# Loading the query weights before the two gMLP weights in a decode-attention kernel

## The chip, the cores and the metric

One core of one Trainium2 chip. The time is the device time of the program in microseconds (us), lower is better. Most executions of one kernel agree within 0.3%, that is about 2 us here.

In this text PE (or TensorE) is the matmul engine, DVE the vector engine, ACT the scalar engine, POOL the engine that here writes a few constants and then only passes on semaphores, and SP the engine whose queue issues the loads. "Load engines" are the 16 DMA engines among which every large load is split.

## The reference, cut to what matters

```python
x = A_x                                             # 1 x 1 x 512
g = sigmoid((x * gate_w).sum(-1))
q = x @ wq                                          # wq: 512 x 4096, 32 heads of 128
scores = q . k_cache * Dh**-0.5                     # k_cache: 32 heads x 16384 x 128
a = (softmax(scores) @ v_cache) @ wo                # v_cache as large; wo: 4096 x 512
z = gelu(x @ w_in)                                  # w_in: 512 x 1792
z1, z2 = halves of z;  z2 = layernorm(z2)
b = (z1 * (w_sp * z2 + b_sp)) @ w_out               # w_out: 896 x 512
out = g * a + (1 - g) * b
```

Everything is bfloat16. The two caches are 134 MB each and all of them must come through the loads once; the arithmetic on one query token is small beside that.

## The kernel before

There are three buffers of 8.4 MB in SBUF. The caches are taken in 16 pairs of heads, K0 to K15 and V0 to V15, each one load of 128 rows of 64 KiB (K0, K15 and V15 are cut into pieces). They go into the buffers in turn, in the order K0, K1, V0, K2, V1, K3, V2 and so on, and load n waits until load n - 3 has been used up. The three setup weights lie in the third buffer, so that V0's load has to wait until the setup is done.

```python
# the small loads, on ACT's queue
act.op(... x_row <- A_x ...); act.op(... gw_row <- gate_w ...)
act.op(... wb_row[0] <- B_w_sp ...); act.op(... wb_row[1] <- B_b_sp ...)
# the setup weights, on SP's queue, ahead of K0
sp.op(lambda e: e.dma_start(out=w_in, in_=B_w_in.rearrange("(p c) f -> p (c f)", c=DC)), inc=(ld_w, 16))
sp.op(lambda e: e.dma_start(out=w_out, in_=B_w_out.rearrange("(p k) n -> p (k n)", k=FhC)), inc=(ld_u, 16))
sp.op(lambda e: e.dma_start(out=wq, in_=A_wq.rearrange("(p c) n -> p (c n)", c=DC)), inc=(ld_q, 16))
# ... (cut) x broadcast, gate, clears of PSUM
dve.op(lambda e: e.memset(ps_all[:, 0:7 * 512], 0.0), mark=True)

# PE's order in the setup:
#   1 gate             waits for the small loads
#   2 gMLP input       waits for ld_w      (pe_gmlp)
#   3 gMLP statistics  waits for DVE, which masks, sums (3.3 us) and squares the result of 2
#   4 queries          waits for ld_q      (pe_queries)
#   5 gMLP output      waits for ld_u      (pe_mixer); its end frees the setup buffer for V0
# ... (cut)

# the loads: load n waits for the user of load n - 3
k_at = [max(2 * i - 1, 0) for i in range(NP)]
v_at = [min(2 * i + 2, 2 * NP - 1) for i in range(NP)]
for n, kind, i in loads:
    wait = [user[n - 3]] if n >= 3 else [w_free] if buf[n % 3] is setup else []
    ...
# user of K_i: the exponentials of pair i (ACT), after DVE's four multiplications by the query
# and PE's sums of the products. user of V_i: PE's product with the probabilities.
```

So K0's end releases K2's load, and K1's end releases V1's load.

The softmax here doesn't subtract the row's maximum and nothing guards it: scores larger than these inputs give would overflow.

## Time and profile before

| | before |
|---|---|
| time, median of 3 runs | 654.57 us (653.9 to 655.1) |
| load queue busy, share of 16 load engines | 99.3% |
| PE, DVE busy | 63%, 52% |
| gMLP input weights landed, first gMLP matmul | 7.6 us, 8.6 us |
| V0's load issued / K0's first multiplication | 31.1 us / 32.2 us |
| V1's load issued | 84.9 us |

The page of the profile of the kernel before: the span, the busy time of the engines, the load queue (packets, MB, share of 16 engines' span), the group of DVE's multiplications (busy us and mean ns; idle time before them and what ended it), and the three setup loads (KB, us from issue to landing).

```profile
span 652.6 us, 7678 instructions
...
PE 412.8 (63%) x2354; PEld 46.3 (7%) x1326; DVE 339.3 (52%) x162; ACT 43.5 (7%) x112; POOL 2.1 (0%) x9
...
q1 hardware_dynamic: 6772, 279.58, 99.3%
...
L560 DVE TENSOR_TENSOR bufs<-bufs,qb x64 | 281.5, 4419 | 168.7 <-DVEq L84 168.7
...
bufs<-in_A_wq_dram SPq DMA_DIRECT2D x1, 4096.0 KB, 18.1
...
bufs<-in_B_w_in_dram SPq DMA_DIRECT2D x1, 1792.0 KB, 7.6
...
bufs<-in_B_w_out_dram SPq DMA_DIRECT2D x1, 896.0 KB, 8.8
```

The load queue is the limit: 99.3% against 63% for the busiest other engine. DVE sits idle for 169 us before its multiplications, in waits for semaphores; the view of waits counts 16 of them, as many as there are K loads.

The timeline of the kernel before, in order: start and duration in us, engine, line, operation, count, and in brackets the idle time before it and what ended it. DVE L312 makes the gate's product, PE L342 starts the gMLP's input, PE L104 with xb is the queries, SP L621 issues cache loads (V0 at 31.13, K2 at 59.38, V1 at 84.87), DVE L560 is the multiplication of K by the query (K0 at 32.20, K2 at 97.33).

```profile
6.86 0.41 DVE L312 TENSOR_TENSOR xg_row<-x_row,gw_row 1x512 bf16<-1x512 bf16 x1 [0.28 <-DMA wb_row<-in_B_b_sp_dram]
...
8.63 0.55 PE L342 MATMUL ps_all<-bufs,xb 128*128 x1
...
23.55 6.61 PE L104 MATMUL ps_all<-bufs,xb 128*64 x32
...
31.13 0.33 SPq L621 DMA_DIRECT2D bufs<-in_A_v_cache_dram  x1
32.20 8.76 DVE L560 TENSOR_TENSOR bufs<-bufs,qb  x2 [0.68 <-DVEq L84]
...
59.38 0.33 SPq L621 DMA_DIRECT2D bufs<-in_A_k_cache_dram  x1
...
84.87 0.33 SPq L621 DMA_DIRECT2D bufs<-in_A_v_cache_dram  x1
...
97.33 8.76 DVE L560 TENSOR_TENSOR bufs<-bufs,qb  x2 [13.12 <-DVEq L84]
```

DVE had been idle for 13.12 us when K2 arrived: at that place the engines are ahead of the loads.

### The profile page before, as it was taken

What the parts mean: (1) busy time and instruction counts of PE and PEld (TensorE: products, weight loads), DVE (VectorE), ACT (ScalarE), POOL (GpSimd) and SP (SyncE); (2) the same over time, 40 slices, a digit from 0 to 9 for tenths busy, and PEclk for the clock granted to TensorE, in tenths of its full rate; (3) what the DMA queues carried; (4) which work ended last, traced back from release to release, by engine and by line L of the source; (5) the groups of instructions that cost most, each with busy time, mean ns of one, the idle gap of its engine ahead of it and who ended that gap; (6) DMA issues with size and microseconds to landing.
All of it is one profiled execution on the core that took longest, in us unless ns stands there. A gap on an engine that the chain in (4) does not pass through costs nothing. (4 is left out here: it accounts for less than half of the span.)

```text
span 652.6 us, 7678 instructions
## 1 busy us (share of the span) xinstructions
PE 412.8 (63%) x2354; PEld 46.3 (7%) x1326; DVE 339.3 (52%) x162; ACT 43.5 (7%) x112; POOL 2.1 (0%) x9
## 2 busy tenths in 40 slices
PE   3455756757376674847657485674738657487767
PEld 0100010000101000010100101000010100001012
DVE  4596708356280745628166470925638083565600
ACT  2101010000001000010100001000010100001011
POOL 1000000000000000000000000000000000000000
PEclk9588986868889687888958789795887979688888
DMA  9999999999999999999999999999999999999997
GB/s 390 444 428 450 438 438 410 450 438 434 414 450 438 426 422 450 438 426 422 446 442 426 422 446 442 426 422 446 434 426 430 446 434 418 438 418 462 414 412 288
DMA packets 6781, 279.60 MB, mean 428 GB/s; under 512 B 760, under 2 KB 1020, under 8 KB 1532
## 3 DMA queue, kind: packets, MB, share of 16 engines
q1 hardware_dynamic: 6772, 279.58, 99.3%
q8 instruction: 1, 0.02, 0.0%
q10 hardware_dynamic: 8, 0.00, 0.0%
HBM read 279.58 MB, written 0.00 MB: 428 GB/s over the span
## 5 line engine op out<-in xcount | busy, mean ns | idle before, releaser
L560 DVE TENSOR_TENSOR bufs<-bufs,qb x64 | 281.5, 4419 | 168.7 <-DVEq L84 168.7
L89 PE MATMUL ps_all<-bufs,ident 128*128 x960 | 268.7, 438 | 0.0
L477 PE MATMUL ps_all<-bufs,ident 128*128 x64 | 28.9, 451 | 152.6 <-PEq L84 152.6
L104 PE MATMUL ps_all<-bufs,p_t 128*8 x1024 | 79.3, 388 | 53.0 <-PEq L84 52.9
L544 DVE TENSOR_REDUCE s_sb<-ps_all 128x64 f32<-128x512 f32 x64 | 44.1, 689 | 98.1 <-DVEq L84 98.1
L573 ACT ACTIVATE p_t<-s_sb 64x256 f32 (+1 forms) x32 | 13.3, 414 | 442.0 <-ACTq L84 441.6
L477 PEld LDWEIGHTS ps_all<-bufs,ident 128*128 128x128 bf16 x64 | 6.3, 99 | 373.3 <-issue 373.3
L104 PEld LDWEIGHTS ps_all<-bufs,p_t 128*8 x1024 | 17.2, 82 | 163.6 <-issue 163.6
L511 PE MATMUL ps_all<-pick,d_sb 128*128 128x2 f32 x128 | 16.8, 253 | 14.8 <-PEq L84 14.8
L511 PEld LDWEIGHTS ps_all<-pick,d_sb 128*128 128x128 f32 x128 | 15.5, 191 | 26.3 <-issue 26.3
L582 ACT COPY d_sb<-ps_all 128x512 f32<-128x512 f32 x16 | 9.4, 586 | 103.7 <-ACTq L84 103.7
L463 PE MATMUL ps_all<-zero,ident 128*128 128x512 bf16 x25 | 10.4, 415 | 0.0
L89 PE MATMUL ps_all<-zero,ident 128*128 128x512 bf16 x32 | 9.5, 379 | 0.0
L587 ACT CAST ps_all<-zero 128x512 f32<-128x512 bf16 x15 | 8.8, 589 | 1.7
L104 PE MATMUL ps_all<-bufs,xb 128*64 x32 | 6.6, 604 | 0.1
L377 PE MATMUL ps_all<-stats,const-float32-1.0 128*128 128x2 f32 x2 | 0.6, 364 | 9.2 <-DVE stats L375 9.2
L656 DVE TENSOR_TENSOR o_sb<-ps_all,rl 128x32 bf16<-128x32 f32 x1 | 0.2, 192 | 11.5 <-PE ps_all L511 11.5
L573 ACT ACTIVATION_READ_ACCUMULATOR p_t<-s_sb (+1 forms) x32 | 5.9, 184 | 0.0
L653 DVE RECIPROCAL rl<-ps_all 128x32 f32<-128x32 f32 x1 | 0.4, 358 | 10.5 <-PE ps_all L532 10.5
L354 DVE TENSOR_TENSOR bufs<-ps_all,ident 128x896 f32<-128x896 f32 x2 | 2.1, 1086 | 4.6 <-PE ps_all L89 4.6
L319 PE MATMUL ps_all<-xgw,const-float32-1.0 1*128 1x3 f32 x2 | 0.6, 358 | 6.1 <-DVE xgw L315 6.1
L89 PE MATMUL ps_all<-bufs,xb 128*128 x12 | 4.4, 494 | 0.0
(73 smaller groups left out, 44.4 us busy)
## 6 DMA issues: line engine op xcount, KB each, us to landing
bufs<-in_A_k_cache_dram SPq DMA_DIRECT2D x4, 4096.0 KB, 34.0
bufs<-in_A_v_cache_dram SPq DMA_DIRECT2D x1, 5120.0 KB, 33.2
bufs<-in_A_wq_dram SPq DMA_DIRECT2D x1, 4096.0 KB, 18.1
bufs<-in_A_wo_dram SPq DMA_DIRECT2D x3, 1024.0 KB, 23.5
bufs<-in_A_v_cache_dram SPq DMA_DIRECT2D x1, 2048.0 KB, 37.8
bufs<-in_B_w_in_dram SPq DMA_DIRECT2D x1, 1792.0 KB, 7.6
bufs<-in_A_v_cache_dram SPq DMA_DIRECT2D x1, 1024.0 KB, 39.8
bufs<-in_B_w_out_dram SPq DMA_DIRECT2D x1, 896.0 KB, 8.8
```

Source lines behind the costliest of these rows:

```text
L89: ins = eng.matmul(out, lhsT=lhsT, rhs=rhs, **flags).ins
L104: ins = eng.matmul(bank[0:m, 0:n], lhsT=lhsT, rhs=rhs, **flags).ins
L319: g_ok = pe.op(lambda e: e.matmul(l_ps[:, 0:3], lhsT=ones_f[0:1, :], rhs=xgw[:, :], start=True, stop=True), wait=[xgw_ok], mark=True)
L354: dve.op(lambda e, h=h, zh=zh: e.tensor_tensor(out=zm[:, 2 * h * ZB:2 * (h + 1) * ZB].rearrange("p (b m k) -> p b m k", b=2, k=FhC), in0=z ...
L463: e.matmul(args[0], lhsT=args[1], rhs=args[2], **flags)
L477: matmul_on(nc, e, lambda: e.matmul(s3, lhsT=ident[:, :], rhs=k3[:, :, 0:W], start=True, **flags), [(kw, 0)])
L511: ins = e.matmul(o2, lhsT=d_sb[:, r * Dh:(r + 1) * Dh], rhs=pick[:, r * 2:(r + 1) * 2], start=False, stop=False, skip_group_check=True)
L544: return e.tensor_reduce(out=s_sb[:, c * QK:(c + 1) * QK], in_=s_ps[c % 2].rearrange("p (j w) -> p j w", w=W), axis=AX.X, op=ALU.add)
L560: e.tensor_tensor(out=k3, in0=k3, in1=qi, op=ALU.mult).then_inc(mul_s, 1)
L573: e.activation(out=p_t[rows, bass.ds(at, NG * 8)].rearrange("p (t c) -> p t c", c=8)[:, :, 4 * s:4 * s + 4], in_=s_sb[rows, :].rearrange(" ...
L582: return e.copy(out=d_sb[:, :], in_=d_ps)
L587: e.copy(out=d_ps, in_=zero[:, :]).then_inc(drn_s, 1)
```

## The change

The intent is in its title: the query weights are the first load, in 32 KiB rows, ahead of the gMLP's input weights (14 KiB rows) and output weights (7 KiB rows). Nothing else moves in the program; each engine but SP has the same instructions in the same order.

```diff
+    sp.op(lambda e: e.dma_start(out=wq, in_=A_wq.rearrange("(p c) n -> p (c n)", c=DC)),
+          inc=(ld_q, 16))
     sp.op(lambda e: e.dma_start(out=w_in, in_=B_w_in.rearrange("(p c) f -> p (c f)", c=DC)),
           inc=(ld_w, 16))
     sp.op(lambda e: e.dma_start(out=w_out, in_=B_w_out.rearrange("(p k) n -> p (k n)", k=FhC)),
           inc=(ld_u, 16))
-    sp.op(lambda e: e.dma_start(out=wq, in_=A_wq.rearrange("(p c) n -> p (c n)", c=DC)),
-          inc=(ld_q, 16))
```

## The prediction

> **What bounds the kernel now.** The loads. The page of the profile puts 99.3% of 16 engines' span on the load queue, 279.6 MB at a mean 428 GB/s; PE is 63% and DVE 52% busy. The Trainium skill ("DMA: Bandwidth & Descriptors", Specifications) gives 435 GB/s as the fabric ceiling; this trace agrees, with 408 to 455 GB/s in 20 us windows. The time is about 1 us before the first bytes, 279.6 MB at that rate, and a tail of 4 to 5 us after the last output weights land (about 648 us by the windows). The chain of waits ends in that tail. Each later load is issued while 11 to 21 us of earlier loads are queued (issue to landing 30.8 us for V, 40.9 us for K, against 19.6 us to move 8.4 MB at 428 GB/s).
>
> **What changes.** No instruction is added or removed; three setup loads trade places. Bytes and packets stay: query weights 4.19 MB in 32 KiB rows, gMLP input weights 1.84 MB in 14 KiB rows, gMLP output weights 0.92 MB in 7 KiB rows. All still precede the first keys, so K0 lands when it did.
>
> Before, the input weights landed at 7.6 us and the first gMLP matmul ran at 8.6 us; the query weights landed at 19.5 us, but the queries waited in PE's order for the gMLP's statistics, until 23.6 us. After, the input weights come behind the query weights: 6.03 MB at 428 GB/s is 14.1 us, plus 1 us to start and the 2.2 us by which the old landings exceeded such a sum: 17.3 us (estimate). The whole setup shifts by about 8.5 us (7 to 10): queries from about 32 us, the setup buffer free at about 40 instead of 31.1, K0's first multiply at about 41 instead of 32.2.
>
> **Is that on the critical path?** No. V0's load, which waits for the setup buffer, is issued at about 40 us, and the queue holds K0 and K1 until about 58.6. K0's multiplies and sums take 25.6 us, as K1's did (58.6 to 84.2), so K0's buffer is released near 68 (was 59.4); its next load is not needed until about 78. K1 starts near 67, ends near 92.5; V1 is issued near 93 (was 84.9), with the queue full until about 97. That is the smallest margin, about 4 us. K2 lands at 97.3, when DVE is already free (it idled 13 us there before), so from the third pair on the pattern is the old one.
>
> **Gain.** Little. Larger rows may fill the engines sooner: 1 to 4 us moved 975 KB where the mean rate gives 1284 KB, 0.7 us lost. But the small rows are still paid for later, and issuing the query weights took SyncE 0.83 us against 0.38, which may start the first bytes up to 0.4 us later. I expect these to nearly cancel.
>
> **Prediction.** 654.5 us, 653.4 to 656.0 eight times in ten. Faster by over 2%: 1%; within 2%: 97.5%; slower by over 2%: 1.5%.
>
> **What the profile would show.** Right: first gMLP matmul near 17 us, first key multiply near 41, DVE's idle time before K2 shrunk from 13 to about 5 us, V1 issued near 93, load queue still 99%, the same tail. Wrong: less DMA in a slice between 80 and 120 us, K2 or V1 landing over 1 us later, or first bytes later.
>
> **What would make it wrong.** Input weights landing past 21 us, which would eat V1's margin and stall the queue once, by the excess; a different spread among the 16 load engines; a start that depends on the first load's row length more than I think. Each is worth a few us at most, below 2% (13 us).

## The result

655.52 us median of 6 runs (654.7 to 656.74), against 654.47 us (653.9 to 655.1, 6 runs) for the kernel before in the same rounds. The ratio is 1.0019, with a 95% interval from 1.0005 to 1.0032. Ratios here and below are the mean time of one kernel's runs over that of the other's of the same rounds, so they are not quite the ratio of the medians quoted beside them. By the 2% rule the two are the same; but the interval leaves 1 out, so there is a small loss to explain. The runs are spread wider (2.0 us) than those of before (1.2 us), but little follows from that: the 11 runs of the kernel before beside experiments 1 to 4 are spread over 2.6 us.

The same lines of the page of the kernel after:

```profile
span 652.9 us, 7678 instructions
...
PE 405.0 (62%) x2354; PEld 46.8 (7%) x1326; DVE 338.8 (52%) x162; ACT 43.5 (7%) x112; POOL 2.1 (0%) x9
...
q1 hardware_dynamic: 6772, 279.58, 99.3%
...
L560 DVE TENSOR_TENSOR bufs<-bufs,qb x64 | 281.5, 4419 | 163.5 <-DVEq L84 163.5
...
bufs<-in_A_wq_dram SPq DMA_DIRECT2D x1, 4096.0 KB, 12.4
...
bufs<-in_B_w_in_dram SPq DMA_DIRECT2D x1, 1792.0 KB, 15.5
...
bufs<-in_B_w_out_dram SPq DMA_DIRECT2D x1, 896.0 KB, 17.3
```

The load queue has the same packets and the same share. The query weights land at 12.4 us, the input weights 15.5 us after their issue at 1.06 us, that is at 16.6 us.

The same places in the timeline of the kernel after (K2 at 68.79 and V1 at 92.88 among the issues; the multiplications of K0 at 40.03 and of K2 at 96.56):

```profile
12.35 0.41 DVE L312 TENSOR_TENSOR xg_row<-x_row,gw_row 1x512 bf16<-1x512 bf16 x1 [5.77 <-DMA wb_row<-in_B_b_sp_dram]
...
17.11 0.55 PE L342 MATMUL ps_all<-bufs,xb 128*128 x1 [2.93 <-DMA bufs<-in_B_w_in_dram]
...
31.60 6.40 PE L104 MATMUL ps_all<-bufs,xb 128*64 x32
...
39.16 0.33 SPq L621 DMA_DIRECT2D bufs<-in_A_v_cache_dram  x1
40.03 8.76 DVE L560 TENSOR_TENSOR bufs<-bufs,qb  x2 [0.68 <-DVEq L84]
...
68.79 0.33 SPq L621 DMA_DIRECT2D bufs<-in_A_k_cache_dram  x1
...
92.88 0.33 SPq L621 DMA_DIRECT2D bufs<-in_A_v_cache_dram  x1
...
96.56 8.76 DVE L560 TENSOR_TENSOR bufs<-bufs,qb  x2 [4.34 <-DVEq L84]
```

The whole setup runs 8.5 us later (17.11 against 8.63), K0's chain 7.8 us later (40.03 against 32.20), and V1's load is issued 8.0 us later (92.88 against 84.87). From K2 on the pattern is the old one: DVE still waited 4.34 us for it, where before it waited 13.12.

Two things in these lines need the trace's records of load packets and completions, which are not in the page. The first is where the loads lost and won time. Each large load is finished by the 16 load engines one by one; these are the first and the last of the 16 completions, in us:

```
load                      before           after
last of the setup loads   17.94 to 19.53   18.25 to 18.76
K1                        56.72 to 58.30   57.03 to 57.54
V0                        76.07 to 77.65   76.38 to 76.88
K2                        95.45 to 97.01   95.73 to 96.24
V1                       114.79 to 116.36  115.08 to 116.54
K3                       134.15 to 135.71  134.44 to 135.90
last output weights      647.70 to 649.15  648.01 to 649.42
```

An 8.4 MB load takes 19.35 us on every engine (433.5 GB/s in all), with hardly any change until the end. In the new order the quickest load engine is 0.3 us later after the setup, but the slowest is 0.77 us earlier: the engines are 0.5 us apart instead of 1.6. That lead of the slowest engine lasts until K2 and is gone at V1.

The second is why. These are the only 64 KiB packets of the whole run that took more than 2.6 us, of 3,712; the median is 2.42 us:

```
kernel after: start us, took ns
95.44 3038
95.45 3824
95.74 2713
kernel before: none
```

They are the first packets of V1 on three of the load engines. V1's load had been issued at 92.88 us, 2.4 to 2.9 us before the engines ended K2's last packets (95.25 to 95.78 us). So the theory to test was that the setup's delay, which was expected to be hidden, used up the lead of V1's load.

### The profile page after: what moved, and what is told of

It reads as the page before. It is cut to its first block, busy times and chain, and to the rows that moved or that the text cites. A ratio compares the mean times of both kernels' runs of the same rounds, so it can differ in the third digit from the quotient of the medians.

```text
span 652.9 us, 7678 instructions
## 1 busy us (share of the span) xinstructions
PE 405.0 (62%) x2354; PEld 46.8 (7%) x1326; DVE 338.8 (52%) x162; ACT 43.5 (7%) x112; POOL 2.1 (0%) x9
## 3 DMA queue, kind: packets, MB, share of 16 engines
q1 hardware_dynamic: 6772, 279.58, 99.3%
## 5 line engine op out<-in xcount | busy, mean ns | idle before, releaser
L560 DVE TENSOR_TENSOR bufs<-bufs,qb x64 | 281.5, 4419 | 163.5 <-DVEq L84 163.5
L89 PE MATMUL ps_all<-bufs,ident 128*128 x960 | 259.1, 424 | 0.0
L477 PE MATMUL ps_all<-bufs,ident 128*128 x64 | 28.4, 443 | 151.9 <-PEq L84 151.4
L104 PE MATMUL ps_all<-bufs,p_t 128*8 x1024 | 80.7, 396 | 53.4 <-PEq L84 53.4
L511 PE MATMUL ps_all<-pick,d_sb 128*128 128x2 f32 x128 | 17.3, 257 | 14.8 <-PEq L84 14.8
L89 PE MATMUL ps_all<-zero,ident 128*128 128x512 bf16 x32 | 9.5, 379 | 0.0
L377 PE MATMUL ps_all<-stats,const-float32-1.0 128*128 128x2 f32 x2 | 0.6, 362 | 9.2 <-DVE stats L375 9.2
## 6 DMA issues: line engine op xcount, KB each, us to landing
bufs<-in_A_wq_dram SPq DMA_DIRECT2D x1, 4096.0 KB, 12.4
bufs<-in_B_w_in_dram SPq DMA_DIRECT2D x1, 1792.0 KB, 15.5
bufs<-in_B_w_out_dram SPq DMA_DIRECT2D x1, 896.0 KB, 17.3
```

What stands on the lines that cost most here:

```text
L89: ins = eng.matmul(out, lhsT=lhsT, rhs=rhs, **flags).ins
L104: ins = eng.matmul(bank[0:m, 0:n], lhsT=lhsT, rhs=rhs, **flags).ins
L477: matmul_on(nc, e, lambda: e.matmul(s3, lhsT=ident[:, :], rhs=k3[:, :, 0:W], start=True, **flags), [(kw, 0)])
L511: ins = e.matmul(o2, lhsT=d_sb[:, r * Dh:(r + 1) * Dh], rhs=pick[:, r * 2:(r + 1) * 2], start=False, stop=False, skip_group_check=True)
L560: e.tensor_tensor(out=k3, in0=k3, in1=qi, op=ALU.mult).then_inc(mul_s, 1)
```

## The experiments

All were timed in five rounds against the kernel before on the same chip. Theory A: V1's load is issued too late for some engines. Theory B: the order of the first loads costs something in itself, for example at the start. Theory C: chance.

This table has the readings of all profiles. "Late" counts V1's first packets over 2.6 us. "Apart" is the distance of the 16 completions of the last setup load, and "last landing" is the last completion of the last output weights. The profiles are single executions; the ratios come from the timed runs. The two are not to be set against each other to the tenth of a us: in the two profiles of the changed kernel the last landing is 0.3 and 0.9 us after that of the kernel before, while the timed loss is 1.2 and 1.9 us, and the profiled execution of experiment 1 was the quickest of its six (654.69 us). Against the new order with V1 in time (648.40 and 648.41 us in experiments 3 and 5) these two landings are 1.0 and 1.6 us late.

| run | V1 issued, us | K2 landed, us | late | apart, us | last landing, us | ratio (95%) |
|---|---|---|---|---|---|---|
| before | 84.87 | 95.45 to 97.01 | 0 | 1.59 | 649.15 | |
| after | 92.88 | 95.73 to 96.24 | 3 | 0.50 | 649.42 | 1.0019 (1.0005 to 1.0032) |
| 1 after, again | 94.08 | 95.74 to 96.22 | 14 | 0.49 | 650.03 | 1.0029 (1.0014 to 1.0044) |
| 2 before, three clears | 96.31 | 95.52 to 96.74 | 15 | 1.22 | 652.03 | 1.0037 (1.0020 to 1.0055) |
| 3 after, statistics late | 92.19 | 95.70 to 96.11 | 0 | 0.47 | 648.40 | 0.9998 (0.9984 to 1.0012) |
| 4 after, five clears | 102.97 | 100.16 to 100.80 | 16 | 0.50 | 658.34 | 1.0175 (1.0155 to 1.0195) |
| 5 after, short sum | 90.50 | 95.70 to 96.20 | 0 | 0.49 | 648.41 | 0.9982 (0.9969 to 0.9995) |
| 6 half of wq first | 87.88 | 95.78 to 96.19 | 0 | 0.42 | 648.40 | 0.9993 (0.9975 to 1.0011) |
| 7 before, two clears | 91.67 | 95.45 to 96.67 | 1 | 1.21 | 648.96 | 0.9998 (0.9980 to 1.0016) |
| 8 before, again | 85.05 | 95.57 to 96.68 | 0 | 1.12 | 648.85 | 0.9992 (0.9978 to 1.0006) |
| 9 half of wq first, again | 87.88 | 95.67 to 96.39 | 0 | 0.71 | 648.71 | 1.0002 (0.9989 to 1.0014) |
| 10 half first, no fillers | 89.25 | 95.75 to 96.23 | 0 | 0.49 | 648.43 | 1.0004 (0.9992 to 1.0017) |
| 11 before, no fillers | 85.18 | 95.61 to 97.05 | 0 | 1.40 | 649.19 | 1.0015 (1.0003 to 1.0027) |
| 12 quarter of wq first | 85.87 | 95.66 to 96.58 | 0 | 0.93 | 648.75 | 1.0002 (0.9990 to 1.0014) |

### 1. The changed kernel again

No edit.

> The changed kernel once more, five rounds against the kernel before. Theory A (the setup runs 8 us later, so V1's load is issued at 92.9 us, when the load engines run dry of K2 at about 95.4 us, and its first rows come late on some engines): ratio 1.001 to 1.003, and again packets of well over 2.6 us (normal 2.42) at about 95 us and nowhere else. Theory B (the order of the first loads itself, long rows first, costs time at the start, for example the first landings 0.3 us later on every engine): ratio the same, but the long packets near 95 us absent or without connection with the end. Theory C (chance): the ratio's interval holds 1.000.

Measured: 655.98 us median (654.69 to 657.91, 6 runs) against 654.34 us (11 runs). The loss is real: two sets of rounds, both intervals above 1, so theory C falls. V1 was issued later than in the first profile, at 94.08 us, and there were 14 late first packets instead of 3. Six of the 14 began only at 96.03 to 96.49 us, when the last engine had been done with K2 since 95.77. One more packet, at 106.6 us, took 2.64 us, so "nowhere else" was not quite met.

Why is the same program 1.2 us later here? The timelines show it. First the kernel after, then this run: PE's first sums of K1 (L89), the multiplication that waits for them (L560), and the issue of V1; then the stretches in which the sums fall, with TensorE's granted clock (PEclk, 1.00 is full speed).

```profile
72.33 4.60 PE L89 MATMUL ps_all<-bufs,ident 128*128 x15
...
77.69 4.42 DVE L560 TENSOR_TENSOR bufs<-bufs,qb  x1
...
92.88 0.41 ACT L573 ACTIVATE p_t<-s_sb 64x256 bf16<-64x256 f32 x1
92.88 0.33 SPq L621 DMA_DIRECT2D bufs<-in_A_v_cache_dram  x1
```

```profile
core 0: us, PE busy (x) PEld busy (x) DVE busy (x) ACT busy (x) POOL busy (x), PEclk, DMA share, GB/s
...
72.00:74.00 2.00, 2.00 (x5) 0.03 (x1) 2.00 (x1) 0.00 (x0) 0.00 (x0) 0.50 1.14 492
74.00:76.00 2.00, 2.00 (x9) 0.00 (x0) 1.78 (x1) 0.00 (x0) 0.00 (x0) 0.81 0.15 66
76.00:78.00 2.00, 2.00 (x11) 0.10 (x1) 0.92 (x2) 0.00 (x0) 0.00 (x0) 1.00 1.14 492
```

```profile
72.11 6.03 PE L89 MATMUL ps_all<-bufs,ident 128*128 x15
...
78.89 4.42 DVE L560 TENSOR_TENSOR bufs<-bufs,qb  x1
...
94.08 0.41 ACT L573 ACTIVATE p_t<-s_sb 64x256 bf16<-64x256 f32 x1
94.08 0.33 SPq L621 DMA_DIRECT2D bufs<-in_A_v_cache_dram  x1
```

```profile
core 0: us, PE busy (x) PEld busy (x) DVE busy (x) ACT busy (x) POOL busy (x), PEclk, DMA share, GB/s
...
72.00:74.00 2.00, 2.00 (x6) 0.00 (x0) 2.00 (x1) 0.00 (x0) 0.00 (x0) 0.50 1.14 492
74.00:76.00 2.00, 2.00 (x7) 0.00 (x0) 1.55 (x1) 0.00 (x0) 0.00 (x0) 0.50 0.46 197
76.00:78.00 2.00, 2.00 (x8) 0.10 (x1) 0.00 (x0) 0.00 (x0) 0.00 (x0) 0.65 0.83 360
```

In this run the clock was still at half from 74 to 76 us, and the first sums took 6.03 us instead of 4.60. The third multiplication of K1 came 1.20 us later, and V1's issue as well. The Trainium skill ("TensorE: Matmul & The Clock Gate", Part 1: The HAM clock gate) says that the clock is set by activity in free-running windows of about 3.4 us, so that one kernel differs from run to run. The traces agree: the first stretches at half clock in these two runs last 3.4, 6.8 or 10.2 us. Between these two profiles the clock moved V1's issue by 1.2 us; that V1's lead is thus a matter of chance within a us or so in the other runs is likely, but they have no profile.

### 2. The old order, with a delay

```diff
     dve.op(lambda e: e.memset(ps_all[:, 0:7 * 512], 0.0), mark=True)
+    for _ in range(3):
+        dve.chain(lambda e: e.memset(ps_all[:, 0:7 * 512], 0.0))
```

> The old load order, with three more clears of PSUM (3 us each) ahead of the gMLP, so that the setup runs about 9 us late as in the changed kernel, V1's load issued near 94 us. Theory A: as slow as the changed kernel or a little slower, ratio 1.002 to 1.004 (1.3 to 2.6 us), long first packets near 95 us. Theory B: ratio 1.000, as the loads are those of before.

Measured: 657.58 us median (655.26 to 659.16), ratio 1.0037. The loads are in the old order, and the loss is there, larger than the changed kernel's, with V1 issued at 96.31 us. The delay alone is enough; theory B is not needed, and cannot explain this run.

Not all of its size belongs to V1, though. The page of this run has a queue that the pages of before and after do not have:

```profile
q14 instruction: 1, 0.01, 0.0%
```

It is one packet of 8 KiB at 636.15 us, as if the three added clears had moved a fetch of instructions into the run. The 16 KiB packet that starts when it ends, at 636.47 us, took 1.27 us instead of 0.61, and the 16 completions, 0.61 us apart before it, are 1.58 us apart after it. So about 1 us of this run's late last landing came from there. Experiments 4 and 7, which have added clears too, have such a packet at 643.05 and 634.30 us; in all other profiles its like comes only after the end of the span. What is V1's own is seen at V1's landing, well before: the last completion is 118.14 us against 116.36, 1.8 us late. And experiment 7, with such a packet and without a late V1, shows no loss.

### 3. The new order, with the setup shortened

The gMLP's statistics (the matmul L377 and all that hangs on it) are put behind the queries, so that the queries do not wait for them. Results are right.

```diff
-    tot_ok = pe.op(...)          # statistics, and DVE and ACT's work after it down to u_ok
-    ...
     pe.raw(pe_queries)
     q_free = [...]
     pe.n += 8 * DC
+    tot_ok = pe.op(...)
+    ...
```

> The new load order, with the gMLP's statistics (PE, DVE and ACT) put behind the queries, which then start about 5 us earlier; right results; V1's load issued near 89.5 us instead of 92.9. Theory A: no long packets near 95 us, time back to that of before or 0.3 to 0.9 us below it (ratio 0.9985 to 1.0005), since the slowest load engine ended the setup loads 0.77 us earlier in the new order. Theory B: still the time of the changed kernel, ratio 1.001 to 1.003.

Measured: 654.6 us median, ratio 0.9998. V1's issue came forward less than expected, to 92.19 us instead of 89.5: here the gMLP's output took 5 us instead of 1 (38.4 to 43.4 us, the granted clock at 0.50, and PE idle between its pairs of matmuls), and PE's first sums of K0 came only after it, at 44.48 us. The interval, 0.9984 to 1.0012, does not quite exclude theory B's least, 1.001; experiment 5 does. Yet 0.7 us was enough in this profile: no late packet, and the last landing is 648.40 us, 0.75 us before that of the kernel before.

### 4. The new order, with more delay

```diff
     dve.op(lambda e: e.memset(ps_all[:, 0:7 * 512], 0.0), mark=True)
+    for _ in range(5):
+        dve.chain(lambda e: e.memset(ps_all[:, 0:7 * 512], 0.0))
```

> The new load order with five more clears of PSUM ahead of the gMLP: setup another 6.5 us later, V1's load issued near 99.5 us, some 4 us after the queue is empty. Theory A: the queue stands still for about 5 us there, and the end moves by as much: ratio 1.008 to 1.011 (5 to 7 us). Theory B: the time of the changed kernel, ratio 1.001 to 1.003, as the order of loads is unchanged.

Measured: 665.76 us median, ratio 1.0175, so 11.4 us by the medians instead of 5 to 7. The direction is theory A's and the size was missed. One reason is that a clear costs 3.9 us with the wait for the one before it, and not 3: V0's load was issued 10.3 us later than in the changed kernel (49.46 against 39.16), where 6.5 was expected. The other is that there are two holes, stretches in which the queue is empty, and not one. Stretches of this run, with the busy time of each engine, the granted clock, the DMA share and GB/s (packets seem to be counted where they start):

```profile
core 0: us, PE busy (x) PEld busy (x) DVE busy (x) ACT busy (x) POOL busy (x), PEclk, DMA share, GB/s
77.00:79.00 2.00, 0.00 (x0) 0.00 (x0) 1.87 (x1) 1.89 (x4) 0.00 (x0) 1.00 0.00 0
79.00:80.00 1.00, 0.00 (x0) 0.00 (x0) 1.00 (x1) 0.41 (x2) 0.00 (x0) 1.00 1.58 524
...
101.00:102.00 1.00, 0.47 (x3) 0.00 (x0) 0.38 (x1) 0.00 (x0) 0.00 (x0) 1.00 0.00 0
102.00:103.00 1.00, 0.44 (x8) 0.14 (x8) 0.84 (x2) 0.54 (x3) 0.00 (x0) 1.00 0.00 0
103.00:104.00 1.00, 0.65 (x12) 0.13 (x8) 1.00 (x1) 0.47 (x2) 0.00 (x0) 1.00 0.97 328
```

No packet starts from 77 to 79 us, because K2's load was issued only at 78.90 us, after V0 had landed (76.3 to 76.8 us): the delay made K0's end late too. No packet starts from 101 to 103 us, because V1's was issued at 102.97 us, after K2 had landed (100.2 to 100.8 us). K2 lands 4.6 us later than in the changed kernel (100.80 against 96.24 us, last engine), V1 8.3 us (124.82 against 116.54), the last output weights 8.9 us (658.34 against 649.42); the last 0.6 us came with the instruction packet told of in experiment 2, at which the completions went from 0.49 to 1.24 us apart.

These holes also give the cost of a start on an empty queue: the first packets begin 0.95 us after the load's issue, and nearly all of these first packets took 2.9 to 3.4 us instead of 2.42.

### 5. The new order, with a shorter setup

```diff
-        in_=zm.rearrange("p (e m k) -> p e k m", e=2, k=FhC), axis=AX.X, op=ALU.add))
+        in_=zm.rearrange("p (e m k) -> p e k m", e=2, k=FhC)[:, :, :, 0:4], axis=AX.X, op=ALU.add))
```

> The changed kernel with a result made wrong on purpose: the gMLP's 3.3 us sum over the masked products reads 4 of 64 columns, so that the setup is some 3 us shorter and V1's load is issued near 90 us, before the margin is gone. Theory A (late V1 is the whole loss): no packet over 2.6 us near 95 us, time at or below that of before; and if the smaller spread among the load engines at the start (0.5 against 1.2 to 1.6 us) is worth anything at the end, ratio 0.998 to 0.9995, otherwise 1.000. Theory B (the order itself costs): ratio 1.001 to 1.003.

Measured: 653.49 us median (652.88 to 653.91), ratio 0.9982; the result is wrong, as intended (only the gMLP's branch). V1 was issued at 90.50 us, no packet was late, and the last landing is 648.41 us. The order is wholly that of the changed kernel, so theory B falls here for the second time: with V1 issued 2.4 us earlier the new order is not slower at all.

### 6 and 9. Half of the query weights first

```diff
-    sp.op(lambda e: e.dma_start(out=wq, in_=A_wq...), inc=(ld_q, 16))
+    wq_src, wq_half = A_wq.rearrange("(p c) n -> p (c n)", c=DC), DC * HDh // 2
+    sp.op(lambda e: e.dma_start(out=wq[:, 0:wq_half], in_=wq_src[:, 0:wq_half]), inc=(ld_q, 16))
     sp.op(lambda e: e.dma_start(out=w_in, ...), inc=(ld_w, 16))
+    sp.op(lambda e: e.dma_start(out=wq[:, wq_half:], in_=wq_src[:, wq_half:]), inc=(ld_q, 16))
     # the queries wait for ld_q at 32
```

> New order with half of the query weights first (16 KiB rows), then the gMLP's input weights, then the other half; right results. Input weights land near 11.5 to 12.5 us, V1's load issued near 88 us. Theory A: no late packets, ratio 0.9985 to 1.0005. Theory B (anything large ahead of the gMLP weights costs): about half of the changed kernel's loss, ratio near 1.001. If the small spread at the start comes from long first rows, it should lie between 0.5 and 1.6 us here.

> Half of the query weights first, run once more, as the first five rounds gave 0.9993 with an interval that holds 1. If the smaller spread of the load engines is worth its 0.75 us at the last landing: ratio 0.998 to 0.9995 again, spread near 0.4 us, V1's load near 88 us, no packets over 2.6 us. If that gain is hidden by the tail on PE, whose clock differs from run to run: 0.9995 to 1.0005.

Measured: 653.82 us and 653.94 us median, ratios 0.9993 and 1.0002. V1 is issued at 87.88 us both times, nothing is late, the last landing is 648.40 and 648.71 us. So the loss of the changed kernel is gone with half of its load still in front. A gain over the kernel before is not shown: both intervals hold 1.

### 7. The old order, with a smaller delay

The edit of experiment 2 with `range(2)`.

> Old load order, two more clears of PSUM: V1's load issued near 91 us, 4 us before the queue runs dry at about 95.3. Theory A with a threshold near 92.5 us: no late packets and ratio 1.000 (0.999 to 1.001), though the setup is 6 us late. If instead any lateness of the setup costs in proportion, ratio near 1.002 to 1.0025 (two thirds of the three clears' 1.0037).

Measured: 654.01 us median, ratio 0.9998 (0.9980 to 1.0016), V1 issued at 91.67 us, one packet at 2.64 us. Together with experiment 2 (1.0037 with one clear, 3.9 us, more) this favours a threshold. The 1.002 to 1.0025 expected of a cost in proportion lies outside the interval. The interval is too wide to rule out a smaller such cost, but its middle is where the threshold puts it.

### 8. The kernel before again

No edit.

> The kernel before against itself: ratio 1.000, within 0.0015 either way; no packets over 2.6 us; V1's load issued near 85 us; spread among the load engines at the start 1.2 to 1.6 us, if that belongs to the old order and is not chance.

Measured: 654.14 us median, ratio 0.9992 (0.9978 to 1.0006). This is how well such a comparison resolves: an equal kernel came out 0.08% off. The load engines were 1.12 us apart, a little less than expected; five profiles of the old order now have 1.59, 1.22, 1.21, 1.12 and 1.40 us, and five of the new order 0.50, 0.49, 0.47, 0.50 and 0.49 us, so the difference belongs to the order.

### 10 and 11. Without the filler matmuls of the tail

The last load landed 0.4 to 0.75 us earlier in experiments 3, 5, 6 and 9 than in the kernel before; the times hardly moved, but for experiment 5. The tail seemed to be PE's, and PE does a filler matmul after each group of output weights, to keep its clock up. Both runs drop it:

```diff
             ins.then_inc(pe.sem, 1)
-            warm(e, 1)
             e.reg_alu(va, va, 2 * WG * D, ALU.add)
```

> The same, without the filler matmul after each group of the output weights (6 of the 0.32 to 0.54 us). If the tail is limited by PE after the last V piece (the chain of waits of before says so), the end comes 0.5 to 1.5 us earlier, ratio 0.9965 to 0.9985, and the chain's tail waits for the last output weights instead; if the fillers keep PE fast enough to pay for themselves, no gain or a loss of some tenths of a us.

> The kernel before without the fillers, to part their share from the order's: if the tail is PE's, ratio 0.998 to 0.9995; last output weights land near 649 us as before. The difference to the run with half of the query weights first is the order's share, 0.5 to 0.8 us if the last landing counts.

Measured: half of the query weights first without fillers 654.05 us, ratio 1.0004; the kernel before without fillers 654.83 us, ratio 1.0015 (1.0003 to 1.0027), a small loss. So the expected gain was wrong. In the kernel before the fillers pay for themselves, if only just; with half of the query weights first the two are not told apart (1.0004 without, 1.0002 with, in experiment 9). In the timelines the last but one group of 8 matmuls with output weights took 1.06 us in the kernel before without fillers and 0.60 us with them.

The tail's clock is seen in the windows from 640 to 648 us: the kernel before, experiment 3 and experiment 5. The columns are start and end, length, busy time of PE, PEld, DVE, ACT and POOL with the number of instructions, granted clock, DMA share, GB/s.

```profile
640.00:644.00 4.00, 3.21 (x23) 1.55 (x20) 0.59 (x3) 1.16 (x2) 0.00 (x0) 1.00 1.01 422
644.00:648.00 4.00, 4.00 (x24) 0.76 (x20) 0.00 (x0) 0.00 (x0) 0.00 (x0) 0.57 0.92 346
```

```profile
640.00:644.00 4.00, 3.22 (x19) 1.91 (x20) 0.60 (x3) 0.43 (x1) 0.00 (x0) 0.58 1.02 424
644.00:648.00 4.00, 4.00 (x24) 0.77 (x20) 0.00 (x0) 0.00 (x0) 0.00 (x0) 0.57 0.95 354
```

```profile
640.00:644.00 4.00, 3.06 (x24) 1.76 (x25) 0.59 (x3) 0.45 (x1) 0.00 (x0) 1.00 1.01 422
644.00:648.00 4.00, 3.79 (x35) 1.31 (x33) 0.00 (x0) 0.58 (x1) 0.00 (x0) 1.00 0.94 350
```

With the clock at 0.58 and 0.57, experiment 3 took 14.3 us from the last piece of V15 (landed at 638.23 us) to the end of its span at 652.6; the kernel before 13.5 us (639.06 to 652.6); experiment 5, at full clock, 12.8 us (638.24 to 651.0). A loading gain of 0.8 us is of the size of this scatter, and hard to see in it. The timed runs fit in part: of the 11 runs of the kernel before beside experiments 1 to 4, the slowest (656.14 us) had the lowest mean granted clock (0.825), and the two quickest (653.54 and 653.65 us) had 0.845. Of the 11 beside experiments 5 to 8, one of the quickest had 0.832 (653.66 us) and one of the slowest 0.843 (655.34 us). The mean clock of a run is not that of its tail, so this stays a likely reading and is not shown.

### 12. A quarter of the query weights first

Experiment 6 with the cut at `HDh`, so that the first load has 8 KiB rows.

> A quarter of the query weights first, in 8 KiB rows. On the spread of the load engines: if long first rows make it small, it is 1.2 us or more here; if the gMLP input weights' load (14 KiB rows) as the first load makes it large, it is 0.4 to 0.5 us here too. V1's load near 86 us, no late packets; ratio 0.998 to 1.000.

Measured: 653.78 us median, ratio 1.0002. The load engines are 0.61 us apart after this first load and 0.92 us after the gMLP's input weights. That is neither of the two answers expected. With half of the weights first, in 16 KiB rows, it was 0.42, 0.71 and 0.49 us. So the rows' length alone does not set the spread, and what does is left open.

## Why the prediction was right or wrong

**Right: the load queue is the bound, and the time hardly moves.** 654.5 us was predicted, 653.4 to 656.0; 655.52 us was measured. The share of the load queue stayed at 99.3%. The windows of 408 to 455 GB/s that the prediction sets beside a ceiling of 435 are coarse: one set of 16 packets of 64 KiB more or less is 52 GB/s in 20 us. The 433.5 GB/s of the loads' regular 19.35 us say it better.

**Right: the size of the setup's shift.** Predicted about 8.5 us; measured 8.48 (first gMLP matmul 17.11 against 8.63). The input weights landed at 16.6 us against an estimate of 17.3. K0's first multiplication was predicted near 41 us and came at 40.03, V1's issue near 93 and came at 92.88, DVE's idle time before K2 about 5 us and was 4.34.

**Wrong: "That is the smallest margin, about 4 us."** This is the step that failed, and it is why the small loss was not foreseen. The issue time was right; the deadline was mis-sized. The stall itself the prediction had named as a risk, but only for input weights that land past 21 us; they landed at 16.6, and packets of V1 were late all the same. The deadline was taken from K2's landing at about 97 us, as the program sees it on the slowest engine. Two terms were missing. The quickest engine is done with K2's packets at 95.25 us, where the 97 us were read from the slowest engine's completion. And a load has to be issued some time before an engine needs it: with 14 of 16 first packets late at an issue 1.2 to 1.7 us ahead of the end of K2's last packets, 3 of 16 late at 2.4 to 2.9 us, and none at 3.2 to 3.6 us (experiment 1, the changed kernel, and experiment 3), the lead needed lies near 3 us. This is an estimate from single profiles and no sharp limit: the three late packets of the changed kernel are not those with the least lead, and experiment 7 had one of 2.64 us at a lead of 3.8 us. So the margin was about 0, not 4 us, and a shift like the 1.2 us of the granted clock in experiment 1 is enough to lose it. Experiment 2 shows that the delay costs without the new order, experiments 3 and 5 that the new order shows no loss without so much delay, and experiment 4 that a larger delay opens a hole in the queue at both places where the margin is small.

**Half right: "I expect these to nearly cancel."** The later start that was feared did not come: the first packets start at 1.03 us in both kernels, and as the first load the query weights took SP 0.39 us to issue, not 0.83. Of the setup loads' last completions, the first is 0.3 us later and the last 0.77 us earlier. The prediction had named a different spread among the load engines as a risk; it turned out as a gain of about 0.5 us at the last landing where V1 is in time: 648.40 to 648.75 us, mean 648.52, in the six such profiles that begin with query weights, and 648.85 to 649.19 us, mean 649.04, in the four of the old order. In the times this gain is not shown: the kernels that have it and give right results lie between 0.9993 and 1.0004.

**Not foreseen, and harmless: the small loads.** In the kernel after, the last of ACT's four small loads landed at 12.25 us instead of 6.76, and the gate's product on DVE waited 5.77 us for it (it is in the timeline above). The Trainium skill ("DMA: Bandwidth & Descriptors", Queues, rings and completion order) says that a load engine takes turns between its queues at whole packets. The trace agrees: the last small loads' packets start at 7.04, 8.26, 9.47, 10.69 and 11.90 us, 1.22 us apart, and a 32 KiB packet took 1.21 us. In the kernel before, beside 14 KiB packets of 0.54 us and then 7 KiB packets of 0.27 us, the steps were 0.5 to 0.6 and then about 0.3 us. The gate was ready before the input weights all the same.

**Not settled.** Experiment 5 came out at 0.9982, its interval below 1, and the right kernels with as much margin did not follow it. Its profile had the tail at full clock, but whether its timed runs did, no run shows. What makes the spread among the load engines smaller in the new order is open as well. No version tried is shown to beat the kernel before.

## What to carry to other kernels

In a kernel that is bound by its loads, a delay of the setup is free only while every later load is still issued early enough; look for the load with the least lead, and take as its deadline the moment when the first load engine runs dry, less the lead that a load needs (about 3 us by the estimate above), and not the moment when the slowest one lands. A change of 8 us off the critical path was hidden except for one place 80 us later. Before a gain below 0.2% is believed, an equal kernel should be run against itself, since with the same last landing (648.40 and 648.41 us) the spans of experiments 3 and 5 differ by 1.5 us here.

## What the Trainium skill lacked or had wrong

- "DMA: Bandwidth & Descriptors", Latency and other measured facts, gives about 600 ns to the first byte of a load issued from SP or ACT, and does not say from when it counts. Here the first packets of a load issued on an empty queue begin 0.95 to 1.03 us after the start of the issuing instruction (about 0.6 us after its end, as it lasts 0.33 to 0.39 us), so the figure fits if it is counted from the end.
- No page says how far ahead of a busy queue's end a load has to be issued so that no load engine waits. Here a lead of 3.2 to 3.6 us was enough, 2.4 to 2.9 us left 3 of 16 engines with a late first packet, 1.2 to 1.7 us left 14.
- No page says that the 16 load engines can keep through a long run the distance that they had after the first loads: 1.6 us at 19.5 us and still 1.5 us at 649 us in the kernel before, where no packet was late.
- The turn-taking at packets ("DMA: Bandwidth & Descriptors", Queues, rings and completion order) lacks its consequence for small loads on a second queue: four loads of 2 to 1,024 bytes took until 12.25 us beside 32 KiB packets, and until 6.76 us beside 14 KiB and 7 KiB packets.
